# Second feed-forward layer: the seven-product form applied to two 512-token blocks at once, with one block's gated values kept in DRAM

## The chip, the cores and the metric

The program runs on one core of one Trainium2 chip. The metric is device time in microseconds (us) of one launch; lower is better. Matrix products run on TensorE (PE in the profile), elementwise work on VectorE (DVE), ScalarE (ACT) and GpSimd (POOL); SyncE (SP) issues nearly all DMAs of the part of the program that the change touches. Each of these engines works off its own instructions in order.

## The reference

```python
x = _attn_ref(x, state)                  # 8 batches, 512 tokens + 32 state rows each
x = x.transpose(...).reshape(4352, 512)  # 8 * 544 rows
g = x @ moe_w_gate; silu = g * (1 / (1 + np.exp(-g)))
x = (silu * (x @ moe_w_val)) @ moe_w_out             # layer 1, d_ff 1536
h = x @ moe2_w_in                                    # layer 2, d_ff 2048
g = h * (1 / (1 + np.exp(-1.702 * h)))
return (g @ moe2_w_out).astype(np.float32)
```

All is float32. The change touches layer 2 alone: `h = x @ w_in`, the gate, and `g @ w_out`, for 4352 rows.

## The kernel before, in words

**Precision.** A float32 operand is cut into a high and a low part (`cut`, L795 to L798: ACT casts the high part, DVE subtracts it for the low part). A product of two cut operands is three matmuls: high by high, low by high, high by low.

**Layer 2, by blocks.** The rows go through in nine blocks, called n here: n=0 holds the 256 state rows, n=1 to n=8 hold 512 tokens each. d_ff is cut into 16 strips f of 128 (`F2`). For each strip the kernel makes h, gates it, cuts the gated value (`to_h`, into one of three h tiles), and puts it on the list `waiting`; `out2` takes the oldest entry and adds its share of `g @ w_out` into four PSUM accumulators of 128 x 512 (`acc0` to `acc3`): 12 matmuls, 512 columns wide (L340 to L342). After the sixteenth strip of a block `evac` copies the accumulators out, two on ACT (L808) and two on DVE (L809), and SP stores them (L1209). The next block takes the same four accumulators.

**The seven products.** For n=0 and n=1 each strip is 12 plain matmuls. For n=2 to n=8 the function `four` makes two strips at once, as a 2 x 2 by 2 x 2 product with seven sub-products instead of eight (a Strassen-Winograd form). Rows of the weights are the two strips of a pair p (0 to 7), the shared dimension of 512 is halved, and the **columns are the two halves of the block's 512 tokens** (Q = 256). Each sub-product is six matmuls of 256 columns (L1230 to L1232), 42 for a pair. DVE and ACT add the seven results together from PSUM (L1240 to L1257), ACT takes the sigmoid (L1254, L1259), DVE multiplies (L1260, L1264). Two `out2` calls stand inside each `four`, after the fourth and after the seventh sub-product, so the output products of a block run between the sub-products of the same or the next block.

**Operands.** The seven token operands of block n+1 (plain quarters and differences of quarters) are made during block n by `x3_step`. Three of the weight operands are sums that were made once, during n=1; they come back from DRAM as chunks `w2c` (`next_chunk`, L1063, 512 KB, three slots), and the 16 strips of `w_out` come back for each block from `w2b` (`next_out`, L1053, 512 KB, three slots, each issued when the strip three places earlier has been used).

**Order.** It is written out by hand: the loops at the end of the program call `four`, `x3_step`, `out2` in sequence, and each engine's instructions stand in that order. Tiles with few buffers set who waits: PSUM has two `gv` and two `at` tiles, SBUF three `wt`, two `sg`, two `xf`, three h tiles, four `raw`.

Of the kernel before, what the change touches and what calls it, by code (L numbers as in the profile page):

```python
# [8 lines left out]
F32 = mybir.dt.float32  # L9
F32R = mybir.dt.float32r  # L10
U32 = mybir.dt.uint32
ACTF = mybir.ActivationFunctionType
ALU = mybir.AluOpType
# [61 lines left out]
def kernel(  # L75
# [24 lines left out]
    B, H, S, D = x.shape  # L100
    NS = state.shape[2]
    DM = H * D
    FF1 = w_gate.shape[1]
    FF2 = w2_in.shape[1]
    P = 128
# [3 lines left out]
    F2 = FF2 // P  # L109
# [6 lines left out]
    v, a, pe, pool_e, sy = nc.vector, nc.scalar, nc.tensor, nc.gpsimd, nc.sync  # L116
# [4 lines left out]
    work = ctx.enter_context(tc.tile_pool(name="work", bufs=2))  # L121
    xp = ctx.enter_context(tc.tile_pool(name="xop", bufs=1))
    dp = ctx.enter_context(tc.tile_pool(name="scratch", bufs=1, space=DRAM))
# [12 lines left out]
    def f32(t):  # L136
        return t.bitcast(F32)
# [17 lines left out]
    units = {}  # L155
    pos = {"dma": 0, "begun": 0, "done": 0, "ahead": 4, "outs": 0, "jobs": 0}
    RAWS = 4
# [155 lines left out]
    def need(key):  # L313
        while pos["done"] <= where[key]:
            w_step()
# [28 lines left out]
    def accs():  # L344
        return [psa.tile([P, 512], F32, name=f"acc{i}", tag=f"acc{i}") for i in range(4)]

    def gv():
        return psg.tile([P, 512], F32, name="gv", tag="gv")
# [3 lines left out]
    def at():  # L352
        if extra:
            extra.append(extra.pop(0))
            if extra[0] != "at":
                return psa.tile([P, 512], F32, name="at", tag=extra[0])
        return pst.tile([P, 512], F32, name="at", tag="at")
# [436 lines left out]
    y1 = {}  # L794

    def cut(h_, l_, src, eng=v):
        a.copy(h_, src)  # L797
        eng.tensor_tensor(l_, src, f32(h_), op=ALU.subtract)  # L798
# [2 lines left out]
        t = pl.tile([P, 2, S], F32R, name="xo", tag=f"x{k}")  # L801
        return t[:, 0, :N], t[:, 1, :N]

    def evac(acc, N):

        for e in range(0, len(acc), 2):
            ev = work.tile([P, 2, 512], F32, name="ev", tag="raw", bufs=RAWS)
            a.copy(ev[:, 0, :N], acc[e][:, :N])  # L808
            v.tensor_copy(ev[:, 1, :N], acc[e + 1][:, :N])  # L809
            yield e, ev  # L810

    def h_tile(n):
        pl = work if n < 2 else x2p
        return pl.tile([P, 2, 512], F32R, name="h", tag=f"h{n}", bufs=1)
# [44 lines left out]
    x2q = None  # L859
# [40 lines left out]
    order2 = [B] + list(range(B))  # L900
    for i, blk in enumerate(order1):
        tail = blk == B
        last = i == NB1 - 1
        N = NT if tail else S
# [26 lines left out]
        acc = []  # L931
# [39 lines left out]
        for f in range(F1):  # L971
# [4 lines left out]
            sg = work.tile([P, 512], F32, name="sg", tag="sg")  # L976
# [57 lines left out]
    Q = S // 2  # L1034
    PAIRS = F2 // 2
    NCH = 3 * PAIRS // 2
    chunks = [dp.tile([P, 2, 2, Q], F32, name=f"w2c{c}") for c in range(NCH)]
    XRAW = (6, 7)
    EXTRA = {0: (8, 9, 10), 1: (11, 12, 13)}

    def slot(f, shape, name, dt=F32R):
        pl, tag = slot2[f]
        return pl.tile(shape, dt, name=name, tag=tag, bufs=1)
# [13 lines left out]

    def next_chunk(load=True):
        c = pos2["chunks"]
        if c < NCH * (len(order2) - 1):  # L1060
            mixed[c] = t = slot(3 + c % 3, [P, 2, 2, Q], "wc")
            if load:
                sy.dma_start(f32(t), chunks[c % NCH])  # L1063
            pos2["chunks"] += 1

    def mixed_at(n, i):

        i += 3 * PAIRS * (n - 1)
        return mixed[i // 2][:, i % 2]
# [3 lines left out]
    def mix_load(p, late=False):  # L1073
        sraw[p] = r = work.tile([P, 2, DM], F32, name="sr", tag="raw", bufs=RAWS)
        for j in range(2):
            if late:
                sy.dma_start(r[:, j, :Q], whole2["i2", 2 * p + j][:, :Q])
            else:
                sy.dma_start(r[:, j, :], whole2["i2", 2 * p + j])
# [3 lines left out]
    def mix_store():  # L1083
        while full:
            c = full.pop(0)
            sy.dma_start(chunks[c], f32(mixed[c]))
# [36 lines left out]
    def mix_step(n, f):  # L1123

        mix_store()
        s = n * F2 + f
        for back, fn in ((2, mix_cut), (1, mix_add), (0, mix_load)):
            p, odd = divmod(s - back - 6, 2)
            if not odd and 0 <= p < PAIRS:
                fn(p)  # L1130
        if s == F2 + 8:
            for _ in range(3):
                next_chunk()
        for back, fn in ((2, late_cut), (1, late_add), (0, lambda p: mix_load(p, True))):
            p = s - back - F2 - 8
            if 0 <= p < PAIRS:
                fn(p)
# [4 lines left out]
    def x3_step(n, f):  # L1142

        if f == 1:
            for j in range(2):
                xraw[j] = r = slot(XRAW[j], [P, 2, S], "xr", F32)
                sy.dma_start(r, y1[order2[n]][j])
        if f < 3:
            return
        b11, b12 = xraw[0][:, :, :Q], xraw[0][:, :, Q:]  # L1150
        b21, b22 = xraw[1][:, :, :Q], xraw[1][:, :, Q:]
        ops = {
            3: (0, b11),
            4: (b11, b12, b11),
            5: (2, b22),
            6: (b12, b22, b12),
            7: (4, b11),
            8: (b11, b22, b11),
            9: (5, b11),
            10: (1, b21),  # L1160
            11: (b21, b11, b21),
            12: (6, b12),
            13: (3, b21),
        }
        op = ops.get(f)
        if op is None:
            return
        if len(op) == 3:
            v.tensor_tensor(op[0], op[1], op[2], op=ALU.subtract)
            return  # L1170
        k, src = op
        if k < 4 and (n % 2 or k < 2):
            t = (xp if n % 2 else x2q).tile([P, 2, 2, Q], F32R, name="xo", tag=f"x{k}")
        elif k < 4:
            t = slot(12 + k, [P, 2, 2, Q], "xo")
        else:
            t = slot(EXTRA[n % 2][k - 4], [P, 2, 2, Q], "xo")
        xs3.setdefault(n, {})[k] = t
        cut(t[:, 0], t[:, 1], src)

    waiting = []
    acc2 = {}
    done2 = {}

    def out2():
        n, f, h = waiting.pop(0)
        blk = order2[n]
        nt = (NT if blk == B else S) // P
        if n not in acc2:
            acc2[n] = accs()[:nt]  # L1190
            done2[n] = 0
        w = outs.pop((n, f)) if n else units["o2", f]
        done2[n] += 1
        for t in range(nt):
            c = slice(t * P, (t + 1) * P)
            mm_acc(acc2[n][t], h[:, 0, c], h[:, 1, c], w[:, 0, :], w[:, 1, :], done2[n] == 1, done2[n] == F2)
        if n:
            next_out()
        if done2[n] == F2:
            for t, ev in evac(acc2.pop(n), DM):  # L1200
                if blk == B:
                    per = P // NS
                    rows = out.rearrange("(b s) m -> b s m", s=SEQ)
                    for j in range(2):
                        b = (t + j) * per
                        sy.dma_start(rows[b : b + per, S:, :], ev[:, j, :])
                else:
                    rows = out[blk * SEQ : blk * SEQ + S, :].rearrange("(p j) m -> p j m", j=J)
                    sy.dma_start(rows[:, t : t + 2, :], ev)  # L1209
# [3 lines left out]
    def to_h(n, f, sg, N):  # L1213
        h = h_tile(count["h"] % 3)
        count["h"] += 1
        cut(h[:, 0, :N], h[:, 1, :N], sg[:, :N])
        waiting.append((n, f, h))

    def wt():
        return work.tile([P, 512], F32, name="wt", tag="wt", bufs=3)  # L1220
# [46 lines left out]
            if i % 2 == 1:  # L1267
                next_chunk()

    for n in range(len(order2)):  # L1270
        N = NT if order2[n] == B else S
        for f in range(F2):
            if n > 1:
                if n == 2:
                    mix_step(n, f)
                if f % 2 == 0:
                    four(n, f // 2)
                if n + 1 < len(order2):
                    x3_step(n + 1, f)
                continue  # L1280
            if n == 0:
                if 1 < f < 6:
                    need(("io"[f % 2] + "2", F2 - 3 + f // 2))
                if f == 8:
                    for _ in range(3):
                        next_out()
            ps = gv()
            mm_in(ps, units["i2", f], xs2[n], N)
            sg = work.tile([P, 512], F32, name="sg", tag="sg")
            a.activation(sg[:, :N], ps[:, :N], ACTF.Sigmoid, scale=1.702)  # L1290
            v.tensor_tensor(sg[:, :N], ps[:, :N], sg[:, :N], op=ALU.mult)
            to_h(n, f, sg, N)
            if n == 0:
                x2_step(1, f, 2)
            else:
                x3_step(2, f)
            mix_step(n, f)
            if len(waiting) > 2:
                out2()
    while waiting:  # L1300
        out2()

# [28 lines left out]
```

## Time and profile before

| | us |
|---|---|
| median of 3 runs | 1491.26 (1490.56 to 1491.71) |
| the profiled execution, its own time | 1492.28 |
| its span, first to last instruction | 1490.5 |
| PE busy in the span | 1467.6 (98%) |
| DVE / ACT / POOL busy | 915.6 / 684.2 / 396.1 |

The profile comes from one execution. Its span is 1.8 us shorter than that execution's time. A busy PE counts a matmul from its start to its modelled end; consecutive matmuls overlap, so how fast they follow one another is read from their start times. The blocks n=3 to n=8, which the change rewrites, fill about the last 500 us of the span; the granted TensorE clock is full there.

### The profile page before, as it was taken

The page shows a single profiled execution, that of the slowest core. Times are in us where ns is not written, and L with a number is a line of the kernel's source. Part 1 is how long each engine was busy: PE and PEld are TensorE (multiplying, and loading weights), DVE is VectorE, ACT ScalarE, POOL GpSimd, SP SyncE. Part 2 cuts the span into 40 slices and gives each one's busy share as a digit, 9 for nine tenths or more (in the row PEclk, how much of TensorE's full clock was granted, in tenths as well). Part 3 has the DMA queues.
Part 4 walks back from the last instruction along what each step waited for, and adds up shares of the span by engine and source line. Part 5 has one row for each costly group of instructions (what it writes and reads, how often), then busy time and mean ns, then how long its engine had stood idle before and what let it go on. Part 6 is the DMA issues. An engine that isn't in the chain of part 4 may idle for free.

```text
span 1490.5 us, 21226 instructions
## 1 busy us (share of the span) xinstructions
PE 1467.6 (98%) x7688; PEld 1193.8 (80%) x7688; DVE 915.6 (61%) x1600; ACT 684.2 (46%) x1247; POOL 396.1 (27%) x325
## 2 busy tenths in 40 slices
PE   7999999999999999999999999999999999999998
PEld 4445677777787777898788889999999999999997
DVE  7985565656678787943344335656565665656554
ACT  6766554555566666654444333333333232323322
POOL 2665221222234445477646330000000000000000
PEclk9999999999999999999999999999999999999999
DMA  7975433333365656425657746565654646574653
GB/s 217 292 248 159 133 99 110 108 125 105 126 189 172 197 170 190 130 100 171 207 189 270 261 147 211 180 232 174 209 198 170 240 159 240 178 240 165 207 183 128
DMA packets 138480, 269.30 MB, mean 181 GB/s; under 512 B 46728, under 2 KB 57992, under 8 KB 138376
## 3 DMA queue, kind: packets, MB, share of 16 engines
q1 hardware_dynamic: 114680, 223.64, 45.5%
q10 hardware_dynamic: 23696, 44.31, 8.9%
q8 instruction: 61, 1.00, 0.3%
q14 instruction: 43, 0.35, 0.1%
HBM read 202.11 MB, written 63.70 MB: 178 GB/s over the span
## 4 chain that ended last, share of the span: by engine, by line
PE 84%; DMA 5%; DVE 4%; ACT 3%; issue 2%; POOL 1%; SPq 0%; ACTq 0%; DVEq 0%; POOLq 0%
PE acc L340 8%; PE acc L341 8%; PE acc L342 8%; PE acc L952 5%; PE acc L954 5%; PE gv L330 5%; PE acc L953 5%; PE gv L331 4%; PE gv L332 4%; DMA xf<-sw 4%; PE gv L1232 4%; PE gv L1231 4%; PE gv L1230 4%; PE at L629 4%; PE at L1230 3%; PE at L1231 3%
## 5 line engine op out<-in xcount | busy, mean ns | idle before, releaser
L798 DVE TENSOR_TENSOR h<-sg,h 128x512 fp32r<-128x512 f32 (+1 forms) x240 | 193.5, 806 | 129.8 <-ACT h L797 128.2
L797 ACT CAST h<-sg 128x512 fp32r<-128x512 f32 (+1 forms) x251 | 149.8, 597 | 170.4 <-DVE sg L1264 80.2
L340 PE MATMUL acc<-wo,h 128*128 128x512 f32 x512 | 200.6, 392 | 0.0
L341 PE MATMUL acc<-wo,h 128*128 128x512 f32 x512 | 200.6, 392 | 0.0
L342 PE MATMUL acc<-wo,h 128*128 128x512 f32 x512 | 199.2, 389 | 0.0
L1254 ACT ACTIVATE sg<-wt 128x512 f32<-128x512 f32 x56 | 35.4, 632 | 299.5 <-DVE wt L1252 299.5
L668 POOL TENSOR_TENSOR xo<-xf,xo 128x512 fp32r<-128x512 f32 x84 | 110.9, 1325 | 231.9 <-ACT xo L667 216.5
L952 PE MATMUL acc<-h,wu 128*128 128x512 f32 (+1 forms) x428 | 165.9, 388 | 0.1
L954 PE MATMUL acc<-h,wu 128*128 128x512 f32 (+1 forms) x428 | 163.8, 383 | 2.0 <-DVE h L798 2.0
L953 PE MATMUL acc<-h,wu 128*128 128x512 f32 (+1 forms) x428 | 163.4, 382 | 0.0
L330 PE MATMUL gv<-a,xo 128*128 128x512 f32 x336 | 137.3, 409 | 0.0
L331 PE MATMUL gv<-a,xo 128*128 128x512 f32 x336 | 133.9, 399 | 0.6 <-POOL xo L668 0.5
L332 PE MATMUL gv<-a,xo 128*128 128x512 f32 x336 | 133.0, 396 | 0.0
L992 DVE TENSOR_TENSOR sg<-gv,sg 128x512 f32<-128x512 f32 (+1 forms) x107 | 70.5, 659 | 83.1 <-PE gv L332 50.7
L342 PEld LDWEIGHTS acc<-wo,h 128*128 128x128 f32 x512 | 96.2, 188 | 20.8
L340 PEld LDWEIGHTS acc<-wo,h 128*128 128x128 f32 x512 | 96.6, 189 | 17.1
L341 PEld LDWEIGHTS acc<-wo,h 128*128 128x128 f32 x512 | 96.6, 189 | 15.8
L1252 DVE TENSOR_TENSOR wt<-wt,gv 128x256 f32<-128x256 f32 x56 | 23.6, 421 | 136.4 <-PE gv L1232 136.4
L952 PEld LDWEIGHTS acc<-h,wu 128*128 128x128 f32 x428 | 80.9, 189 | 22.1 <-issue 6.1
L977 ACT ACTIVATE sg<-gv 128x512 f32<-128x512 f32 (+1 forms) x108 | 61.5, 570 | 80.1 <-PE gv L332 77.0
L954 PEld LDWEIGHTS acc<-h,wu 128*128 128x128 f32 x428 | 80.9, 189 | 21.1 <-DVE h L798 5.5
L1232 PE MATMUL gv<-xo,wu 128*128 128x256 f32 x336 | 95.4, 284 | 0.0
(178 smaller groups left out, 3438.6 us busy)
## 6 DMA issues: line engine op xcount, KB each, us to landing
wo<-w2b SPq DMA_DIRECT2D x128, 512.0 KB
wc<-w2c SPq DMA_DIRECT2D x84, 512.0 KB
xf<-sw ACTq DMA_DIRECT2D x84, 256.0 KB
raw<-in_moe_w_out_dram SPq DMA_DIRECT2D x28, 512.0 KB
sw<-qs ACTq DMA_DIRECT2D x24, 512.0 KB
sw<-qs ACTq DMA_DIRECT2D x24, 384.0 KB
xn<-in_x_dram SPq DMA_DIRECT2D x16, 512.0 KB
y<-ev SPq DMA_DIRECT2D x16, 512.0 KB
```

The source lines that it names most:

```text
L330: pe.matmul(ps, wh, xh, start=k == 0, stop=False)
L331: pe.matmul(ps, wl, xh, start=False, stop=False)
L332: pe.matmul(ps, wh, xl, start=False, stop=k == len(pairs) - 1)
L340: pe.matmul(ps, lh, rh, start=first, stop=False)
L341: pe.matmul(ps, lh, rl, start=False, stop=False)
L342: pe.matmul(ps, ll, rh, start=False, stop=last)
L797: a.copy(h_, src)
L798: eng.tensor_tensor(l_, src, f32(h_), op=ALU.subtract)
L952: pe.matmul(ps, w[:, 0, c], h[:, 0, :N], start=f == 0, stop=False)
L953: pe.matmul(ps, w[:, 1, c], h[:, 0, :N], start=False, stop=False)
L954: pe.matmul(ps, w[:, 0, c], h[:, 1, :N], start=False, stop=f == F1 - 1)
L1232: pe.matmul(ps, w[:, 0, c], x_[:, 1, kt], start=False, stop=kt == 1)
```

## The change

Blocks n=3 to n=8 go through as three pairs of blocks (`DUOS`); n=0, 1 and 2 stay as they were. In the new `four_duo` the **columns of the 2 x 2 product are the two blocks of a pair**, so each of the seven sub-products has six matmuls of 512 columns, and one call yields two strips for both blocks. The first block's gated values go to `to_h` and `out2` as before. The second block's are written to DRAM (`keep`, 256 KB each, L1339); after the eighth call `rest_of_duo` reads them back (L1386), cuts them, and runs the second block's sixteen `out2` with no sub-products between them. The token operands are made by `duo_step` on 1024 columns at a time (`x3_step` stays for n=2): for the first pair during n=2, for the others during `rest_of_duo`. The chunks of weight sums are read once for a pair of blocks. From n=2 on, `evac` uses tiles of another pool.

```diff
+            if late_out:
+                ev = x2q.tile([P, 2, 512], F32, name="ev", tag=f"x{e // 2}")
+            else:
+                ev = work.tile([P, 2, 512], F32, name="ev", tag="raw", bufs=RAWS)
...
+    DUOS = [(3, 4), (5, 6), (7, 8)]
...
-        if c < NCH * (len(order2) - 1):
+        if c < NCH * (2 + len(DUOS)):
...
+    HOME = {0: ("x0", "x1"), 5: ("x2", "x3"), 4: (6, 7), 6: (11, 12), 3: (13, 8), 1: (9, 10), 2: (14, 15)}
+    DUO_STEPS = [
+        (0, "11"),
+        ("11", "12", "11"),
...
+    def duo_load(j):
+
+        for k in range(2):
+            for c, n in enumerate(DUOS[j]):
+                r = work.tile([P, 2, S], F32, name="xr", tag="raw", bufs=RAWS)
+                sy.dma_start(r, y1[order2[n]][k])
...
+    def duo_step(i):
+
+        op = DUO_STEPS[i]
+        if len(op) == 3:
+            to, x_, y_ = (quarter[q] for q in op)
+            v.tensor_tensor(to, x_, y_, op=ALU.subtract)
+            return
...
+        cut(*parts, src)
...
+    def four_duo(j, p):
...
+        def prod(ps, w, k):
+            xh, xl = duo[k]
+            for kt in range(2):
+                c = slice(kt * P, kt * P + P)
+                pe.matmul(ps, w[:, 0, c], xh[:, kt], start=kt == 0, stop=False)
+                pe.matmul(ps, w[:, 1, c], xh[:, kt], start=False, stop=False)
+                pe.matmul(ps, w[:, 0, c], xl[:, kt], start=False, stop=kt == 1)
+            return ps
...
+        def keep(f, t, sg):
+            v.tensor_tensor(t, t, sg, op=ALU.mult)
+            held_h[nb, f] = d = dp.tile([P, S], F32, name=f"h_{nb}_{f}")
+            sy.dma_start(d, t)
...
+        ps = prod(gv(), s4, 2)
+        add_(one[1], ps, one[1], op=ALU.add)
+        if waiting:
+            out2()
+        to_h(na, 2 * p + 1, s_odd, S)
+        v.tensor_tensor(s_even, one[0], s_even, op=ALU.mult)
+        to_h(na, 2 * p, s_even, S)
+        sg = gated(one[1])
+        keep(2 * p, one[1], sg)
+        for i in range(3 * p + 3 * PAIRS * (j + 2), 3 * p + 3 + 3 * PAIRS * (j + 2)):
+            if i % 2 == 1:
+                next_chunk()
+
+    def rest_of_duo(j):
...
+        def read(s):
+            loaded.append(wt())
+            sy.dma_start(loaded[-1], held_h[nb, order[s]])
+
+        read(0)
+        read(1)
+        for s in range(F2):
+            if s + 2 < F2:
+                read(s + 2)
+            to_h(nb, order[s], loaded.pop(0), S)
+            if j + 1 < len(DUOS) and 0 < s <= len(DUO_STEPS):
+                duo_step(s - 1)
+            if len(waiting) > 2:
+                out2()
...
+                if f == 4:
+                    duo_load(0)
+                if 4 < f < 13:
+                    duo_step(f - 5)
...
+    for j in range(len(DUOS)):
+        for p in range(PAIRS):
+            four_duo(j, p)
+            if p == 4 and j + 1 < len(DUOS):
+                duo_load(j + 1)
+        rest_of_duo(j)
```

The change moves instructions at the place where a block's accumulators are handed to the next block. ACT before, where n=3 ends inside the first `four` of n=4: `h` casts are L797, `ev` copies L808.

```order
1047 L797 CAST h_8952<-sg_8931 128x512
1048 L1240 COPY wt_8959<-gv_8961 128x256
1049 L1254 ACTIVATE sg_9021<-wt_8960 128x512
1050 L1259 ACTIVATE sg_9031<-wt_8959 128x512
1051 L808 COPY ev_9048<-acc0_8269 128x512
1052 L808 COPY ev_9052<-acc2_8271 128x512
1053 L797 CAST h_9056<-sg_9021 128x512
```

ACT now, where n=3 ends in `rest_of_duo` of the first pair: `h_9908` and `h_9927` are the first two strips of n=4, cast from tiles that were read back; `xo_9930` is a token operand of the next pair of blocks; the `ev` copies are L811.

```order
1104 L797 CAST h_9890<-sg_9861 128x512
1105 L1333 ACTIVATE sg_9893<-wt_9788 128x512
1106 L797 CAST h_9908<-wt_9902 128x512
1107 L797 CAST h_9927<-wt_9904 128x512
1108 L797 CAST xo_9930<-xr_9551 128x1024
1109 L811 COPY ev_9948<-acc0_9133 128x512
1110 L811 COPY ev_9952<-acc2_9135 128x512
1111 L797 CAST h_9958<-wt_9906 128x512
```

The two `ev` copies of the finished block stood behind sigmoids of the running `four`; they now stand behind two casts whose inputs are DMA reads and one cast of 1024 columns. DVE has the same order.

SP's queue at the same place, before: `wo` are strips of `w_out`, `wc` chunks of weight sums, `xr` token rows.

```order
348 L1063 DMA wc_8955<-w2c1_6955 128x1024
349 L1063 DMA wc_8957<-w2c2_6956 128x1024
350 L1053 DMA wo_9004<-w2b0_134 128x1024
351 L1053 DMA wo_9046<-w2b3_137 128x1024
352 L1209 DMA out_0_dram<-ev_9048 128x1024
353 L1209 DMA out_0_dram<-ev_9052 128x1024
```

SP's queue now: `h_4_14` is strip 14 of n=4 on its way to DRAM, and the `wt` rows are the reads of strips 1, 0, 3 and 2.

```order
398 L1057 DMA wo_9884<-w2b1_135 128x1024
399 L1339 DMA h_4_14_9896<-wt_9788 128x512
400 L1067 DMA wc_9898<-w2c1_6955 128x1024
401 L1067 DMA wc_9900<-w2c2_6956 128x1024
402 L1386 DMA wt_9902<-h_4_1_9010 128x512
403 L1386 DMA wt_9904<-h_4_0_9087 128x512
404 L1386 DMA wt_9906<-h_4_3_9131 128x512
405 L1057 DMA wo_9923<-w2b0_134 128x1024
406 L1386 DMA wt_9925<-h_4_2_9204 128x512
407 L1057 DMA wo_9946<-w2b3_137 128x1024
408 L1213 DMA out_0_dram<-ev_9948 128x1024
```

The first read stands behind the write of the last strip and behind two chunks; in the third pair of blocks no chunk is left to load, and the two `wc` rows are missing there.

## Rows read from the trace of the kernel before

**Rows 1.** The page: its head, and part 1 (busy us by engine).
```profile
span 1490.5 us, 21226 instructions
PE 1467.6 (98%) x7688; PEld 1193.8 (80%) x7688; DVE 915.6 (61%) x1600; ACT 684.2 (46%) x1247; POOL 396.1 (27%) x325
```

**Rows 2.** Windows: PE, PEld, DVE, ACT, POOL busy, clock, DMA share, GB/s.
```profile
860.00:885.00 25.00, 25.00 (x112) 20.71 (x111) 9.19 (x13) 8.36 (x17) 7.23 (x8) 1.00 0.48 157
1000.00:1400.00 400.00, 400.00 (x2511) 362.65 (x2510) 242.16 (x482) 128.17 (x232) 0.00 (x0) 1.00 0.58 197
```

**Rows 3.** Timeline of SP's issues in n=1, and at ends of n=2, n=7.
```profile
864.44 0.32 SPq L1053 DMA_DIRECT2D wo<-w2b  x1
...
886.20 0.32 SPq L1053 DMA_DIRECT2D wo<-w2b  x1
...
986.68 0.86 SPq L1209 DMA_DIRECT2D out_dram<-ev  x2
...
1407.36 0.86 SPq L1209 DMA_DIRECT2D out_dram<-ev  x2
```

**Rows 4.** Timeline of PE (start, us): in n=4 of layer 2, then in layer 1.
```profile
1081.82 0.28 PE L1230 MATMUL gv<-xo,wc 128*128 128x256 f32 x1
...
1083.61 0.40 PE L340 MATMUL acc<-wo,h 128*128 128x512 f32 x1
...
564.00 0.40 PE L330 MATMUL gv<-a,xo 128*128 128x512 f32 x1
...
565.41 0.39 PE L952 MATMUL acc<-h,wu 128*128 128x512 f32 x1
```

**Rows 5.** Groups of ACT and DVE, 905 to 1400 us: busy, mean ns.
```profile
L798 DVE TENSOR_TENSOR h<-sg,h 128x512 fp32r<-128x512 f32 x95 | 65.8, 692 | 64.5 <-ACT h L797 64.5
L797 ACT CAST h<-sg 128x512 fp32r<-128x512 f32 x94 | 58.4, 621 | 68.8 <-DVE sg L1264 67.3
...
L1244 DVE TENSOR_TENSOR wt<-at,wt 128x256 f32<-128x256 f32 x48 | 20.4, 425 | 8.0 <-PE at L1232 3.6
...
L1240 ACT COPY wt<-gv 128x256 f32<-128x256 f32 x48 | 17.6, 366 | 2.0 <-PE gv L1232 2.0
...
L808 ACT COPY ev<-acc 128x512 f32<-128x512 f32 x10 | 5.8, 578 | 2.3 <-PE acc L342 1.8 <-issue 0.5
```

**Rows 6.** Timeline of DVE, then ACT, behind the program's last sub-product.
```profile
1479.65 0.69 DVE L798 TENSOR_TENSOR h<-sg,h 128x512 fp32r<-128x512 f32 x1 [0.69 <-ACT h L797]
1480.26 0.69 DVE L1264 TENSOR_TENSOR sg<-wt,sg 128x512 f32<-128x512 f32 x1
1481.69 0.69 DVE L798 TENSOR_TENSOR h<-sg,h 128x512 fp32r<-128x512 f32 x1 [0.74 <-ACT h L797]
...
1481.04 0.62 ACT L797 CAST h<-sg 128x512 fp32r<-128x512 f32 x1 [1.42 <-DVE sg L1264]
```

**Rows 7.** Timeline of DVE, then PE: a strip's low part, and its use.
```profile
1090.55 0.69 DVE L798 TENSOR_TENSOR h<-sg,h 128x512 fp32r<-128x512 f32 x1 [0.69 <-ACT h L797]
...
1094.59 0.39 PE L342 MATMUL acc<-wo,h 128*128 128x512 f32 x1
```

**Rows 8.** Chain that ended last: start, us, the DMA waited for (256 KB each).
```profile
72.43 2.84 DMA raw<-in_moe_w_gate_dram
...
783.29 3.56 DMA sr<-w2i
```

**Rows 9.** Windows early in the program (columns as in Rows 2).
```profile
14.00:16.00 2.00, 2.00 (x6) 0.68 (x4) 1.85 (x4) 2.00 (x4) 0.69 (x2) 1.00 1.05 385
```

**Rows 10.** Windows of PE alone: busy, count, granted clock, DMA share, GB/s.
```profile
78.00:80.00 2.00, 1.05 (x2) 1.00 0.13 45
80.00:82.00 2.00, 2.00 (x7) 0.69 0.87 242
82.00:84.00 2.00, 2.00 (x6) 0.50 0.87 231
84.00:86.00 2.00, 2.00 (x8) 0.96 0.99 355
472.00:474.00 2.00, 0.51 (x3) 1.00 0.43 152
```

More of the change, by code (lines that the diff above doesn't have):

```diff
@@ L802, in x_tiles, with evac @@
         return t[:, 0, :N], t[:, 1, :N]
-    def evac(acc, N):
+    def evac(acc, N, late_out=False):
         for e in range(0, len(acc), 2):
-            ev = work.tile([P, 2, 512], F32, name="ev", tag="raw", bufs=RAWS)
+            if late_out:
+                ev = x2q.tile([P, 2, 512], F32, name="ev", tag=f"x{e // 2}")
+            else:
+                ev = work.tile([P, 2, 512], F32, name="ev", tag="raw", bufs=RAWS)
             a.copy(ev[:, 0, :N], acc[e][:, :N])
@@ L1199, in out2 @@
         if done2[n] == F2:
-            for t, ev in evac(acc2.pop(n), DM):
+            for t, ev in evac(acc2.pop(n), DM, n > 1):
                 if blk == B:
@@ L1268, in four @@
                 next_chunk()
-    for n in range(len(order2)):
+    HOME = {0: ("x0", "x1"), 5: ("x2", "x3"), 4: (6, 7), 6: (11, 12), 3: (13, 8), 1: (9, 10), 2: (14, 15)}
+    DUO_STEPS = [
+        (0, "11"),
+        ("11", "12", "11"),
+        (4, "11"),
+        ("11", "22", "11"),
+        (5, "11"),
+        ("12", "22", "12"),
+        (6, "12"),
+        ("11", "11", "21"),
+        (3, "11"),
+        (1, "21"),
+        (2, "22"),
+    ]
+    duo = {}
+    quarter = {}
+    held_h = {}
@@ new lines, in duo_load @@
+    def duo_load(j):
[3 more added lines that the diff above has]
+                sy.dma_start(r, y1[order2[n]][k])
+                quarter[f"{k + 1}{c + 1}"] = r
+    def duo_step(i):
[4 more added lines that the diff above has]
+            return
+        k, src = op[0], quarter[op[1]]
+        parts = []
+        for home in HOME[k]:
+            if isinstance(home, str):
+                parts.append(xp.tile([P, 2, S], F32R, name="xo", tag=home))
+            else:
+                parts.append(slot(home, [P, 2, S], "xo"))
+        cut(*parts, src)
+        duo[k] = parts
@@ new lines, in four_duo, with gated @@
+    def four_duo(j, p):
+        na, nb = DUOS[j]
+        w0, w1 = units["i2", 2 * p], units["i2", 2 * p + 1]
+        def prod(ps, w, k):
[6 more added lines that the diff above has]
+            return ps
+        def gated(src):
+            sg = work.tile([P, 512], F32, name="sg", tag="sg")
+            a.activation(sg, src, ACTF.Sigmoid, scale=1.702)
+            return sg
+        def keep(f, t, sg):
+            v.tensor_tensor(t, t, sg, op=ALU.mult)
+            held_h[nb, f] = d = dp.tile([P, S], F32, name=f"h_{nb}_{f}")
+            sy.dma_start(d, t)
+        add_ = v.tensor_tensor
+        s2, s1, s4 = (mixed_at(3 + j, 3 * p + i) for i in range(3))
+        one = [wt(), wt()]
+        two = [work.tile([P, DM], F32, name="xf", tag="xf", bufs=2) for _ in range(2)]
+        ps = prod(gv(), w0[:, :, :Q], 0)
+        a.copy(one[0], ps)
+        ps = prod(at(), s2, 5)
+        add_(one[1], ps, one[0], op=ALU.add)
+        pb = prod(gv(), s1, 4)
+        ps = prod(at(), w1[:, :, :Q], 6)
+        add_(two[0], ps, one[1], op=ALU.add)
+        add_(two[1], pb, two[0], op=ALU.add)
+        add_(one[1], pb, one[1], op=ALU.add)
+        sg = gated(two[1])
+        keep(2 * p + 1, two[1], sg)
+        if waiting:
+            out2()
+        ps = prod(gv(), w1[:, :, Q:], 3)
+        add_(two[0], two[0], ps, op=ALU.subtract)
+        s_odd = gated(two[0])
+        ps = prod(at(), w0[:, :, Q:], 1)
+        add_(one[0], ps, one[0], op=ALU.add)
+        s_even = gated(one[0])
+        v.tensor_tensor(s_odd, two[0], s_odd, op=ALU.mult)
+        ps = prod(gv(), s4, 2)
+        add_(one[1], ps, one[1], op=ALU.add)
+        if waiting:
+            out2()
[7 more added lines that the diff above has]
+                next_chunk()
@@ new lines, in rest_of_duo @@
+    def rest_of_duo(j):
+        nb = DUOS[j][1]
+        order = [s ^ 1 for s in range(F2)]
+        loaded = []
+        def read(s):
[10 more added lines that the diff above has]
+            if len(waiting) > 2:
+                out2()
@@ L1271 @@
+    for n in range(3):
         N = NT if order2[n] == B else S
@@ L1273 @@
             if n > 1:
-                if n == 2:
-                    mix_step(n, f)
+                mix_step(n, f)
                 if f % 2 == 0:
                     four(n, f // 2)
-                if n + 1 < len(order2):
-                    x3_step(n + 1, f)
+                if f == 4:
+                    duo_load(0)
+                if 4 < f < 13:
+                    duo_step(f - 5)
+                if f == F2 - 1:
+                    for i in range(8, len(DUO_STEPS)):
+                        duo_step(i)
                 continue
```

## The prediction

> **What bounds the kernel now.** I read the page first: the span is 1490.5 us and PE is busy for 98% of it [rows 1]; the profiled execution took 1492.28 us, so 1.8 us lie around the span, and it stands 1.0 us above the median of 1491.26. Next the windows over the part that the change rewrites: from 1000 to 1400 us PE is busy for all 400, DVE for 242, ACT for 128, DMA at a share of 0.58 [rows 2]. Nothing is waited for on PE there, so what counts is how fast matmuls follow one another, and then every new place where PE waits. The timeline gives the paces. In n=7 SP stores the block before 420.68 us later than it did in n=3 (1407.36 less 986.68, five blocks) [rows 3]: **84.14 us a block**, for 336 matmuls of 256 columns and 192 of 512. Fifteen steps of 256 columns take 1083.61 - 1081.82 = 1.79 us, 0.1193 each [rows 4]. The pace of 512 columns in an unbroken stream stands in n=1, whose strips are 12 plain matmuls and 12 of `out2`, all 512 wide, from the same kinds of tiles, with PE busy throughout [rows 2]: four strips from 864.44 to 886.20 [rows 3], 5.44 us for 24 matmuls, **0.2267 each**. Two steps of 256 cost 0.2386, so the wide form is cheaper by 5% a column. The 84.14 us also show that the narrow stream taxes its neighbours: 336 x 0.1193 = 40.1 leaves 44.0 for 192 wide matmuls, 0.2294 each.
>
> **What the change removes.** Six blocks cost 6 x 84.14 = 504.8 us. Each pair of blocks becomes 8 x 42 = 336 products and 2 x 192 output matmuls, 720 in all, every one 512 wide: 3 x 720 x 0.2267 = 489.6. **PE gains 15.2 us** if it never waits. The DVE and ACT instructions on PSUM results halve in number and double in width; they had room (242 of 400) and get more. Half the chunk loads go; 48 writes and 48 reads of 256 KB come.
>
> **Inside `four_duo`** I charge nothing. A pair of strips now gives PE 66 x 0.2267 = 15.0 us, DVE 11 adds and multiplies and 2 low parts at 0.69 (13 x 0.69 = 9.0), ACT 7 instructions at about 0.62. Each PSUM tile is free before its next use, with a 5.4 us stretch of four sub-products and 2.7 us of `out2` between. If that cover failed it would show as a wait of a few tenths in each of 24 calls, up to 7 us.
>
> **During n=2** DVE and ACT get `duo_step` in place of `x3_step`, twice as wide. A strip's low part is ready at 1090.55 + 0.69 = 1091.24 and first used at 1094.59 [rows 7]: 3.35 us of cover, including a narrow x step. Width adds some 0.5 us to each instruction (below), two or three of them between uses, with a cast in their chain: up to 3 us. It still fits, barely. I take 0; bounds 0 and 4 us (half a us in each of eight calls).
>
> **The hand-over inside a duo** is the new cost. Call T the end of the last sub-product of the eighth `four_duo`. Before, a block's last `out2` was followed on PE by sub-products, and the copies of the accumulators ran under them. Now PE has three `out2` of the first block left, 36 x 0.2267 = 8.16 us, and then needs the second block's first strip and the freed accumulators.
> - DVE after T: the add of the last result (about T+0.2 to T+0.9), a low part and a multiply at steps of 0.61 (1479.65 to 1480.26 [rows 6]) to T+2.1; ACT casts strip 14 in 0.62 with 0.1 before it [rows 6], T+2.8; DVE its low part and the `keep` multiply, T+4.1. The write of strip 14 goes out at T+4.2, and SP, which is in order, comes to the two chunks and the reads only then: at 0.4 an issue, read 0 at T+5.5.
> - A single 256 KB transfer took 2.84 us from issue to landing, one behind another of its size 3.56 [rows 8]. At the best rate here, 385 GB/s [rows 9], 256 KB move in 0.68 and 512 KB in 1.36, so 2.16 of the 2.84 is lag. Write, two chunks and read 0 are 1.57 MB: T + 4.2 + 2.16 + 4.1 = T+10.4; read 1 lands at T+11.1.
> - ACT then casts strips 1 and 0 (to T+11.7), the 1024-wide `xo`, and only then copies `acc0`. 366 ns at 256 columns and 621 at 512 [rows 5] make 1.1 us at 1024 (bound: twice 0.62); the copy is 0.58 [rows 5], so `acc0` is free at T+13.35. PE waits 13.35 - 8.16 = 5.2 us. DVE (425 ns at 256, 692 at 512 [rows 5], so about 1.2 at 1024) copies `acc1` to T+14.65, 0.65 after PE wants it. **5.85 us each in the first two duos, 11.7.**
> - In the third, no chunk and no `xo` stand ahead: read 0 lands at T + 4.2 + 2.16 + 1.36 = T+7.7, read 1 at T+8.4, `acc0` is free at T+9.75: **1.6 us.**
>
> Sum 13.3. Its bounds: 3 us, if the reads were always in time and only the casts and copies counted (about 1 each), and 19, if the queue drained at 200 GB/s, nearest 1000 to 1400 us [rows 2]. I take 13.3 because the lag and the rate come from loads of this very size.
>
> **The rest of `rest_of_duo`.** Each 2.72 us step moves 512 KB of `w_out` and 256 KB of h, 289 GB/s, under the 385 seen. ACT needs 0.62 + 1.1 and DVE 0.69 + 1.2 a step at most. No wait charged.
>
> **The clock.** PE idle for 5 us can lower it. Early on, PE was busy for 1.05 of the 2 us from 78 to 80; the granted clock then went 0.69, 0.50, 0.96 [rows 10], which is 3.4 us at half speed (2.4 to 1.2 GHz). From 472 to 474, busy 0.51 of 2, nothing fell. Waits of 5.2 us are far longer than either, so I expect a fall after each of the first two and none after 1.6 us. 3.4 us at half speed lose at most 1.7; part of it passes while PE waits, so 1.3 each, **2.6 us** (bounds 0 and 6.8, if it stays low twice as long). The Trainium skill says of this ("TensorE: Matmul & The Clock Gate", Part 1) that the throttled state is the default and activity releases it; rows 10 show both outcomes. By that rule the term stays; without it the sum would be 2.6 us lower.
>
> **Sum.** -15.2 + 13.3 + 2.6 = +0.7 us: the profiled execution would be 1493.0, the median **1492.0**.
>
> **Rivals.**
> - *The transfers keep ahead, and the clock holds: faster.* If read 0 does not queue behind the two chunks (2 x 1.36 = 2.7 us earlier in two duos, 5.4) and the clock doesn't fall (2.6), the time is 1492.0 - 8.0 = 1484. For it: the share of 0.58 leaves the engines idle at times, and 472 to 474 passed without a fall. Against it: SP's order puts the chunks ahead, and all go through one queue. 0.17.
> - *The width pays little: slower.* In layer 1 six products of 512 columns took 565.41 - 564.00 = 1.41, 0.235 each [rows 4]. If `four_duo`'s 1008 products had that pace, they would cost 8.4 us more: 1500. It decides from about 0.229 a step upward. Against it: n=1 has the same weights and tiles as `four_duo`, at 0.2267. 0.13. The Trainium skill's formula for back-to-back matmuls ("TensorE: Matmul & The Clock Gate", "Back-to-back issue gap": columns / 2.4 + 2.5 ns) points the same way: 109.2 and 215.8 ns, by which 24 calls would save only about 2.6 us (an estimate by that page) and the time would be near 1505. The traces' 119.3 and 226.7 ns disagree with it.
> - *`rest_of_duo` is bound by its transfers: slower by far.* At the 200 GB/s of n=3 to n=7 [rows 2] a step would take 3.9 us instead of 2.72, 48 steps 57 us: 1549. Against it: that rate is what was asked for, at a share of 0.58. 0.05.
>
> **Chances.** My forecast 0.55 (own range 1488 to 1495.5); faster rival 0.17; little pay 0.13; transfer-bound 0.05; the remaining 0.10 is a longer low clock or waits in n=2 and `four_duo`, 1494 to 1500. The range of eight in ten, 1486 to 1499, takes in most of these. About 0.2%, 3 us, is what can be told from no change here. Faster: 0.05 of mine and 0.15 of the rival, 0.20. Slower: 0.08 of mine, 0.13, 0.05 and 0.05, 0.31. Within: 0.49.
>
> **What would show it.** Products L1326 to L1328 stepping at 0.227 and 15.0 us a call; PE idle before the first L340 of n=4 and n=6 for about 5 us and released by ACT's `ev` copy L811, of n=8 for 1.6; after the first two a stretch at clock 0.50; n=2 still at 84 us. I am wrong if PE steps at 0.235 there, if the waits are under 3 us or over 8, or if waits recur inside `rest_of_duo`.

## Result, and the profile after

The changed kernel takes **1499.91 us** (median of 5 runs, 1497.56 to 1502.95) against 1491.26 for the kernel before (5 runs, 1489.96 to 1491.71): a ratio of **1.0058**, 95% interval 1.0047 to 1.0069. It is slower by 8.65 us. The prediction was 1492.0 with a range of 1486 to 1499, so the time lies just outside, and 7.9 us above the forecast. The profiled execution took 1498.6 us.

The page of the kernel after, its head and its table of busy time (us, share, instructions), answers to [rows 1]:

```profile
span 1496.8 us, 19040 instructions
PE 1458.8 (97%) x6680; PEld 1144.1 (76%) x6680; DVE 897.2 (60%) x1399; ACT 677.5 (45%) x1202; POOL 396.6 (26%) x325
```

PE has 1008 matmuls less (each two narrow ones became one wide one) and is busy for 8.8 us less, yet the span is 6.3 us longer. So PE stands idle, or steps more slowly, for more than the products saved. Spans also differ outside the change: in the profile of before the clock fell at 81 us [rows 10], in this one it did not fall there, and the store of block n=1 came 1.8 us earlier. From that store, where the changed part begins, to the last store the two profiles read as follows (SP's timeline, kernel after):

```profile
900.74 0.85 SPq L1213 DMA_DIRECT2D out_dram<-ev  x2
...
1491.87 1.69 SPq L1213 DMA_DIRECT2D out_dram<-ev  x2
```

That is 591.13 us; in the trace of before the same two issues stand at 902.58 and 1485.39, 582.81 us apart. The changed part is 8.3 us longer, which agrees with the 8.65 of the medians.

First, the products. The windows of the kernel after, with columns as in [rows 2], while n=2 makes operands for the first duo and then over six calls of `four_duo`:

```profile
905.00:980.00 75.00, 75.00 (x456) 66.96 (x456) 48.38 (x86) 26.80 (x42) 0.00 (x0) 1.00 0.62 216
1000.00:1090.00 90.00, 90.00 (x398) 74.53 (x398) 51.30 (x78) 25.26 (x43) 0.00 (x0) 1.00 0.55 182
```

SP's timeline there shows the writes of the second block's even strips, one for each call.

```profile
1057.55 0.32 SPq L1339 DMA_DIRECT2D h<-xf  x1
1072.51 0.32 SPq L1339 DMA_DIRECT2D h<-xf  x1
1087.47 0.32 SPq L1339 DMA_DIRECT2D h<-xf  x1
```

PE is never idle in these windows, and a call with its 66 matmuls takes 14.96 us: 0.2267 each, the pace taken from n=1 [rows 3]. So the gain is real. What eats it stands in the table of PE's waits (us in total, times, longest), of which the kernel before has nothing in this stretch [rows 2]:

```profile
PE acc L340 <- ACT ev L811: 15.0, 3, 6.2
PE acc L340 <- DMA wo<-w2b: 0.6, 1, 0.6
```

Three waits for the accumulator's copy, one in each duo. PE's timeline around the first, then the first matmul after each of the others:

```profile
1099.10 0.39 PE L342 MATMUL acc<-wo,h 128*128 128x512 f32 x1
1105.70 0.79 PE L340 MATMUL acc<-wo,h 128*128 128x512 f32 x1 [6.21 <-ACT ev L811]
1106.29 0.63 PE L341 MATMUL acc<-wo,h 128*128 128x512 f32 x1
1106.72 0.63 PE L342 MATMUL acc<-wo,h 128*128 128x512 f32 x1
...
1109.14 0.40 PE L342 MATMUL acc<-wo,h 128*128 128x512 f32 x1
1109.37 0.39 PE L340 MATMUL acc<-wo,h 128*128 128x512 f32 x1
...
1276.98 0.79 PE L340 MATMUL acc<-wo,h 128*128 128x512 f32 x1 [6.00 <-ACT ev L811]
...
1446.09 0.50 PE L340 MATMUL acc<-wo,h 128*128 128x512 f32 x1 [2.79 <-ACT ev L811]
```

The bracket says what ended the idle time. The second column shows a further loss: behind the wait a matmul takes 0.63 us instead of 0.39, and starts are 0.43 apart (1106.29, 1106.72) instead of 0.23 (1109.14, 1109.37). That is the clock. Windows of the same place, all engines, with the granted clock third from the end:

```profile
1098.00:1100.00 2.00, 1.49 (x7) 0.91 (x5) 0.00 (x0) 0.00 (x0) 0.00 (x0) 1.00 0.91 332
1100.00:1102.00 2.00, 0.00 (x0) 0.00 (x0) 0.00 (x0) 0.00 (x0) 0.00 (x0) 1.00 1.02 398
1102.00:1104.00 2.00, 0.00 (x0) 0.00 (x0) 0.38 (x1) 1.02 (x2) 0.00 (x0) 0.50 1.01 398
1104.00:1106.00 2.00, 0.30 (x1) 0.30 (x2) 1.75 (x3) 2.00 (x4) 0.00 (x0) 0.50 0.40 78
1106.00:1108.00 2.00, 2.00 (x5) 1.35 (x5) 2.00 (x4) 0.65 (x2) 0.00 (x0) 0.50 0.97 365
1108.00:1110.00 2.00, 2.00 (x8) 1.58 (x8) 1.35 (x2) 0.00 (x0) 0.00 (x0) 0.79 1.02 401
```

From 1100 to 1102 no engine computes at all and the DMA engines are full at 398 GB/s: everything waits for the queue. The clock is at half (1.2 GHz) from 1102.0, 6.8 us long, and PE works in the last 3.1 of them. At the second hand-over the records show 6.8 us from 1276.1, nearly all of it with PE at work again (it restarts at 1276.98); at the third 3.4 us from 1446.7. PE's own windows, with the clock after the count:

```profile
1272.00:1278.00 6.00, 1.02 (x3) 0.84 0.86 325
1278.00:1284.00 6.00, 6.00 (x17) 0.59 0.87 290
1446.00:1450.00 4.00, 3.91 (x10) 0.59 0.88 275
```

Why the first wait is as long as it is stands in two more timelines, SP's and then ACT's:

```profile
1088.19 6.21 SPq L1057 DMA_DIRECT2D wo<-w2b  x2
1095.35 0.32 SPq L1339 DMA_DIRECT2D h<-wt  x1
1095.71 0.94 SPq L1067 DMA_DIRECT2D wc<-w2c  x2
1096.75 2.30 SPq L1386 DMA_DIRECT2D wt<-h  x3
```

```profile
1102.97 1.24 ACT L797 CAST h<-wt 128x512 fp32r<-128x512 f32 x2 [8.44 <-DMA wt<-h]
1104.12 1.04 ACT L797 CAST xo<-xr 128x1024 fp32r<-128x1024 f32 x1
1105.07 1.07 ACT L811 COPY ev<-acc 128x512 f32<-128x512 f32 x2
```

T, the end of the last sub-product, is about 1091.2. The last write goes out at T+4.1, the chunks and the reads behind it, and ACT can cast the first strip read back at 1102.97, 6.2 us after that read's issue. Two casts and the 1024-wide one stand ahead of the copies of the accumulators, which PE finished with at 1099.5.

Adding up every start-to-start distance on PE from 880 us on, beyond its own pace (0.2267 and 0.1195), the kernel before loses 3.2 us and the kernel after 23.9: waits 15.6, the slow steps behind the three hand-overs 6.5 (1.65, 2.95 and 1.9), n=2 0.5, and 1.3 in small pieces. With the 15.2 gained this is +8.7. Strictly, the 0.5 us that the kernel before loses in n=1 and n=2 has to come off (the other 2.7 of its 3.2 lie in the six blocks and are in the 15.2 already). That leaves +8.2, close to the 8.3 between the two stretches from store to store.

### The profile page after: what moved, and what is told of

The parts are those of the page before. It is cut to its first block, busy times and chain, and to the rows that moved or that the text cites. A ratio compares the mean times of both kernels' runs of the same rounds, so it can differ in the third digit from the quotient of the medians.

```text
span 1496.8 us, 19040 instructions
## 1 busy us (share of the span) xinstructions
PE 1458.8 (97%) x6680; PEld 1144.1 (76%) x6680; DVE 897.2 (60%) x1399; ACT 677.5 (45%) x1202; POOL 396.6 (26%) x325
## 4 chain that ended last, share of the span: by engine, by line
PE 81%; DMA 7%; DVE 5%; ACT 3%; issue 2%; POOL 1%; SPq 1%; ACTq 0%; POOLq 0%; DVEq 0%
PE acc L340 8%; PE acc L341 8%; PE acc L342 8%; PE gv L330 5%; PE acc L957 5%; PE acc L955 5%; PE gv L331 5%; PE acc L956 5%; PE gv L332 4%; DMA xf<-sw 3%; PE at L629 3%; PE gv L1326 3%; PE gv L1327 3%; PE gv L1328 3%; PE at L1326 2%; PE at L1327 2%
## 5 line engine op out<-in xcount | busy, mean ns | idle before, releaser
L340 PE MATMUL acc<-wo,h 128*128 128x512 f32 x512 | 203.0, 396 | 15.6 <-ACT ev L811 15.0
L798 DVE TENSOR_TENSOR h<-sg,h 128x512 fp32r<-128x512 f32 (+1 forms) x192 | 162.3, 845 | 81.7 <-ACT h L797 80.0
L797 ACT CAST h<-sg 128x512 fp32r<-128x512 f32 (+1 forms) x203 | 120.0, 591 | 138.6 <-DVE sg L995 71.1
L340 PEld LDWEIGHTS acc<-wo,h 128*128 128x128 f32 x512 | 97.5, 190 | 38.8 <-ACT ev L811 16.3
L342 PEld LDWEIGHTS acc<-wo,h 128*128 128x128 f32 x512 | 97.4, 190 | 21.2 <-DVE h L798 0.4
L341 PEld LDWEIGHTS acc<-wo,h 128*128 128x128 f32 x512 | 97.8, 191 | 19.2
L1333 ACT ACTIVATE sg<-xf 128x512 f32<-128x512 f32 x48 | 30.4, 633 | 178.1 <-DVE xf L1352 113.5
L957 PEld LDWEIGHTS acc<-h,wu 128*128 128x128 f32 x428 | 80.5, 188 | 22.5 <-DVE h L798 7.1
L955 PEld LDWEIGHTS acc<-h,wu 128*128 128x128 f32 x428 | 80.6, 188 | 21.8 <-issue 6.1
L956 PEld LDWEIGHTS acc<-h,wu 128*128 128x128 f32 x428 | 80.6, 188 | 15.6 <-POOL wu L251 0.3
L330 PEld LDWEIGHTS gv<-a,xo 128*128 128x128 f32 x336 | 63.2, 188 | 30.6 <-issue 18.2
```

The costliest lines, as they stand in the source:

```text
L330: pe.matmul(ps, wh, xh, start=k == 0, stop=False)
L340: pe.matmul(ps, lh, rh, start=first, stop=False)
L341: pe.matmul(ps, lh, rl, start=False, stop=False)
L342: pe.matmul(ps, ll, rh, start=False, stop=last)
L955: pe.matmul(ps, w[:, 0, c], h[:, 0, :N], start=f == 0, stop=False)
L956: pe.matmul(ps, w[:, 1, c], h[:, 0, :N], start=False, stop=False)
```

## Experiments

Theory A, the prediction's own: the loss is the hand-over (copies of the accumulators queued behind casts that wait for the read-back), and the clock that falls because PE is idle there. Rival B: the loss is in the DMA queue itself, so that mending the order on ACT only makes the next transfer, the strips of `w_out`, the one that is late. All ratios are against the kernel before, run on the same chip: median 1492.01 us for the first four, 1492.4 for the last two. Each experiment's own note has its own theories A and B.

**The accumulators copied before anything that waits.** All of the first block's `out2` run ahead of the loop, so `evac` stands before the casts.

```diff
         read(1)
+        while waiting:
+            out2()
         for s in range(F2):
```

> The two out2 calls left of the first block, and with them the copies of its accumulators, are written ahead of the casts of the strips that were read back. Theory A (order): PE's waits of 6.2, 6.0 and 2.8 us are made of two parts, the landing of read 0 and the casts that stand ahead of the copies. Then only read 0 and one cast are left: 4.2, 4.2 and 1.9 us, released by the cast (L797) and not by the copy (L811), and the time falls by 4.7 us of waits and 0 to 3 us of low clock, to 1492 to 1495. Theory B (the read alone decides, the copies come in time anyway): waits and time as in the changed kernel, 1499 to 1501.

1497.23 us, ratio 1.0035 (1.0023 to 1.0047). ACT's timeline, and the table of PE's waits:

```profile
1101.29 0.59 ACT L811 COPY ev<-acc 128x512 f32<-128x512 f32 x1 [2.96 <-PE acc L342]
...
1107.41 0.62 ACT L797 CAST h<-wt 128x512 fp32r<-128x512 f32 x1 [4.18 <-DMA wt<-h]
```

```profile
PE acc L340 <- ACT h L797: 12.4, 4, 4.8
```

The copies now run as soon as PE is done, and PE waits for the cast instead, that is for the read. So the order on ACT was worth about 1.5 us in each of the first two duos, and the transfer the rest. In the third duo the wait shrinks to 1.17 us, but a new one of 2.17 us comes up some steps later. The time lies between the two theories: the waits fell by 3.2 us in all and not by 4.7, and the waits of 4.8 and 4.3 us are still followed by 6.8 us at half clock each, the one of 2.17 by 3.4, so nothing is saved there. (The profiled execution took 1500.69 us, the second slowest of the 12; the trace shows more loss than the median has.)

**The chunks of the next duo later.** The two chunk loads that stand ahead of the reads move to the fourth step of the loop.

```diff
+        if p < PAIRS - 1:
+            chunks_of(j, p)
...
+            if s == 3:
+                chunks_of(j, PAIRS - 1)
```

> The two chunk loads that stand ahead of read 0 in SP's queue are issued later, in the fourth step of rest_of_duo. Theory A (one queue, served in order): read 0 lands 2.5 to 3 us earlier in the first two pairs of blocks, whose waits shrink from 6.2 and 6.0 to about 3.3 us; the third (no chunks there) stays at 2.8. Time 1492 to 1495. Theory B (reads are served beside the chunks, and the lag is the write to DRAM ahead of them): waits unchanged, 1499 to 1501.

1496.11 us, ratio 1.0023 (1.0011 to 1.0035). The table of PE's waits:

```profile
PE acc L340 <- ACT ev L811: 9.6, 3, 3.9
PE acc L340 <- DMA wo<-w2b: 3.6, 3, 1.6
```

The first two waits fall to 3.35 and 3.91, by 2.9 and 2.1 us: the two chunks were worth about what they take on the queue (2.7 by the prediction's rate). But 3.6 us of waits for `w_out` appear: 1.32 and 0.68 behind the place where the chunks were put, and 1.60 in the third duo, which has no chunks. So theory A is right about the reads, but the time is 1.1 us above its range: the queue is late with something else, as rival B says.

**PE kept busy through the wait.** Unread 512-column matmuls (26, 26 and 11) into a free PSUM tile, issued just before the second block's first strip. They compute nothing that is used.

```diff
+            if s == 1:
+                ps = gv()
+                reps = 11 if j == 2 else 26
+                for r in range(reps):
+                    pe.matmul(ps, units["i2", 0][:, 0, :P], duo[2][0][:, 0], start=r == 0, stop=r == reps - 1)
```

> Between the last out2 of the first block and the first out2 of the second, PE gets 26, 26 and 11 matmuls of 512 columns whose result nobody reads (5.9, 5.9 and 2.5 us), so that it works where it waited. Theory A (the clock falls because PE idles there): no stretch at clock 0.50 in layer 2, the wait at the place under 1 us, and the time falls by the 6 us or so that PE now loses at half speed, to 1492 to 1495, with less spread between runs. Theory B (the clock falls for another reason, or costs nothing here): 1499 to 1501.

1496.24 us, ratio 1.0031 (1.002 to 1.0042). PE's windows over the first two hand-overs:

```profile
1098.00:1104.00 6.00, 6.00 (x28) 1.00 0.95 326
1104.00:1110.00 6.00, 5.53 (x23) 1.00 0.85 310
1272.00:1278.00 6.00, 5.88 (x27) 1.00 0.84 314
1278.00:1284.00 6.00, 5.58 (x24) 1.00 0.97 342
```

The clock stays at 1.00 through all three hand-overs, though the data come as late as before: the first strip read back is cast 5.9 us after its read's issue, against 6.2. Over whole executions the mean granted clock was 0.994 to 0.998 in these 12 runs and 0.989 to 0.992 in the five of the changed kernel. So the clock fell because PE was idle, not because of anything else in this stage. Its fall costs 0.0058 - 0.0031 of the time, about 4 us, and by the two intervals anything from 2 to 6. From the trace it is 5.4: the kernel loses 4.2 us beyond its pace, its 63 extra matmuls cost 63 x 0.2267 = 14.3, and 23.9 - 18.5 = 5.4. The time is 1.2 us above theory A's range, and the spread between runs did not shrink (6.1 us over 12 runs, 5.4 over the five).

**The strips made last used first.** Strips 15 and 14 of the second block stay in SBUF and are the first two that it uses; the other 14 go through DRAM. Nothing then has to come back at the hand-over.

```diff
+            if f >= F2 - 2:
+                held_h[nb, f] = t
+                return
...
+        for f in strips(nb)[:2]:
+            to_h(nb, f, held_h[nb, f], S)
+            out2()
+        for s in range(F2 - 2):
```

> The second block's last two strips (15 and 14) stay in SBUF and are the first that rest_of_duo casts and uses; the other fourteen are written and read back as before, and are needed 5.4 us later. Theory A (the hand-over is all that stands between the 15 us gain of the wide products and the clock): no wait over 1 us on PE at the three places, no fall of the clock, 1475 to 1479, faster than the kernel before by 12 to 16 us. Theory B (waits move into the next steps of rest_of_duo, because reads and w_out strips share the queue): PE waits again for reads or strips there, 1485 to 1496.

1487.09 us, ratio **0.9965** (0.9952 to 0.9978): faster than the kernel before. No hand-over is at half clock. What is left, in the table of waits, then SP's timeline at the first hand-over:

```profile
PE acc L340 <- DMA wo<-w2b: 6.6, 5, 2.0
```

```profile
1097.30 0.89 SPq L1074 DMA_DIRECT2D wc<-w2c  x2
1098.29 0.92 SPq L1396 DMA_DIRECT2D wt<-h  x2
1099.64 3.04 SPq L1064 DMA_DIRECT2D wo<-w2b  x2
1102.77 0.86 SPq L1220 DMA_DIRECT2D out_dram<-ev  x2
```

The wait for the read-back and all three falls of the clock are gone, as theory A said, so both were due to the hand-over. But the time lies in theory B's range, 8 us above A's, and B's sign is there too: 6.6 us of waits for strips of `w_out`, up to 1.96 long. At the first two hand-overs their loads were issued behind 1 MB of chunks and 512 KB of reads, and the next ones stand behind the stores of the first block's result; in the third duo, without chunks, one wait of 1.79 us comes some steps later. The queue of rival B is the second limit, under the first.

**The same, with the transfers spread.** On top of the last kernel, the first block's two stores are issued in steps 4 and 6 of the loop, the two chunk loads in steps 8 and 10.

```diff
+                    if n > 2 and n % 2 == 1:
+                        put_off.append((rows[:, t : t + 2, :], ev))
+                    else:
+                        sy.dma_start(rows[:, t : t + 2, :], ev)
...
+            if s in (4, 6):
+                sy.dma_start(*put_off.pop(0))
+            if s == 8 or s == 10:
+                next_chunk()
```

> As the kernel with the last two strips first (e4), and the bulk transfers are taken out of the hand-over: the first block's two output stores are issued in the fifth and seventh step of rest_of_duo's loop, the two chunk loads in the ninth and eleventh. In e4 PE still waited 6.6 us in all, released by w_out strips that had queued behind chunks, stores and reads. Theory A (the queue is backed up only at the hand-over, and drains later at its 290 GB/s of 400): these waits go, under 1 us is left in all, and the time is 5 to 7 us below e4's, ratio to the kernel before 0.991 to 0.993. Theory B (the queue has no room anywhere in rest_of_duo): the waits move to the later steps, ratio as e4's, 0.995 to 0.998.

1481.92 us (1477.78 to 1484.19), ratio **0.9922** (0.9906 to 0.9938): by the medians 10.5 us faster than the kernel before, by the ratio 11.6. By the two ratios that is some 20 us faster than the changed kernel. Its table of waits, and a window of 45 us over PE's first hand-over:

```profile
PE acc L340 <- DMA wo<-w2b: 2.0, 5, 0.8
PE acc L340 <- ACT h L797: 0.5, 1, 0.5
```

```profile
1090.00:1135.00 45.00, 43.91 (x191) 35.14 (x189) 28.70 (x35) 19.37 (x28) 0.00 (x0) 1.00 0.84 286
```

PE is idle for 1.1 us of these 45, at full clock, while the DMA engines move 286 GB/s. The ratio is in theory A's range, but 2.5 us of waits remain where it allowed 1: 2.0 for `w_out`, in the later steps where the second store and the chunks now stand, and 0.5 in n=2. Of the 15.2 us that the wide products gain, 10.5 arrive.

**No read-back at all.** The changed kernel, with the casts reading a part of the weights that lies in SBUF instead of strips from DRAM. It leaves out the second block's true values; writes, chunks, `w_out` and stores stay.

```diff
-        read(0)
-        read(1)
         for s in range(F2):
-            if s + 2 < F2:
-                read(s + 2)
-            to_h(nb, order[s], loaded.pop(0), S)
+            to_h(nb, order[s], f32(units["i2", 0][:, 0, :]), S)
```

> The changed kernel without the reads of the second block: rest_of_duo casts a tile that lies in SBUF (a part of the weights) instead of the strips, so the second block's output is not that of the reference; the writes to DRAM stay, and so does the order of casts and copies. Theory A (the transfers behind SP's queue are the whole loss, the wide products give their 15 us): no wait over 0.5 us at the three places, no low clock in layer 2, ratio to before 0.989 to 0.991. Theory B (part of the loss is in four_duo, in the 1024-column casts or in the order of the copies): waits of 1 us and more remain, ratio 0.993 or above.

1485.04 us, ratio 0.9953 (0.9936 to 0.9971). PE's waits:

```profile
PE acc L340 <- DMA wo<-w2b: 3.4, 2, 1.9
```

With the reads gone PE never waits for ACT or DVE: the copies, casts and 1024-wide steps by themselves cost nothing, so the causes that theory B named here are out. The clock does not fall in layer 2. What is left are 1.5 and 1.9 us for `w_out` at the two hand-overs that have chunks and none at the third, which has none. So theory A's "no wait over 0.5 us" failed as well, and the ratio is 0.004 above its range: rival B's share of the loss, the queue, stays without any read-back.

The traces (one execution each) and the ratios of all seven kernels agree within 3.1 us: the loss beyond PE's own pace less 15.2 (and plus 14.3 for the extra matmuls) gives +8.7 for the changed kernel, then +7.0, +6.5, +3.3, -6.5, -9.1 and -9.5 us in the order of the experiments; the ratios give +8.7, +5.2, +3.4, +4.6, -5.2, -11.6 and -7.0. Three of the gaps have a plain reason in part: the profiled executions of the first and second experiments took 3.5 and 2.1 us more than their medians, that of the last 2.7 less.

## Why the prediction was wrong, by its own steps

- **The products: right.** 0.2267 us each and 14.96 us a call, as predicted; the gain of 15.2 closes the sum above. The rival in which width pays little is out, and with it the formula of the Trainium skill ("TensorE: Matmul & The Clock Gate", "Back-to-back issue gap"; the section gives it for isolated matmuls) as a guide to this stream: it gives 215.8 ns where the changed kernel, with a weight load for every matmul, steps at 226.7. One slip in the working changes nothing: the store at 1407.36 falls in n=8, not in n=7, which is what makes it five blocks.
- **Inside `four_duo`, n=2, and the rest of `rest_of_duo`: nearly right.** No wait in `four_duo`; n=2 cost 0.5 us, inside its bounds of 0 to 4. The 1024-wide instructions were sized well: 1.04 us for the cast above, against 1.1. The steady part of `rest_of_duo` shows PE busy throughout at 288 GB/s, against 289 predicted, so the transfer-bound rival is out as well:

```profile
1112.00:1137.00 25.00, 25.00 (x111) 20.33 (x110) 16.86 (x18) 10.36 (x14) 0.00 (x0) 1.00 0.89 288
```

- **The hand-over: place, releaser and order right, size 2 us short.** 13.3 was predicted, 15.0 measured, and 0.6 for `w_out` in the third duo. Up to the write (T+4.1 against T+4.2) the working holds; the read then landed 1.3 us later than it said (cast at T+11.8 against T+10.5). The sum of what drains ahead of the read left out the strip of `w_out` issued at 1094.08, the second of SP's pair at 1088.19, but by the sum's own rate and lag that moves the landing by 0.1 us only (1094.08 + 2.16 + 5.45 = 1101.7 against 1101.6). What the sum had wrong is the rate: it took 385 GB/s throughout, and the windows show 309 from 1096 to 1098 and 332 from 1098 to 1100, some 0.7 us of the 1.3; the rest is open. The waits were 6.2, 6.0 and 2.8 us against 5.85, 5.85 and 1.6. That the first two agree so well is partly luck: 0.65 of the 5.85 was a second wait, for DVE's copy, which does not show. PE at half clock came to `acc1` at 1107.14, just after the copy was done (about 1107.0); with PE kept busy, at full clock, two such waits of 0.41 and 0.42 us come up. So the part that was forecast for ACT's copy was 5.2 and measured 6.2 and 6.0. And the bound of 19 for a queue at 200 GB/s comes to 22 to 24 by its own steps.
- **The clock: the step that failed.** "I expect a fall after each of the first two and none after 1.6 us. 3.4 us at half speed lose at most 1.7 [...] so 1.3 each, 2.6 us." The third wait, 2.8 us long, brought a fall too, and the first two lasted 6.8 us, not 3.4. The slow steps cost 6.5 us by the start times, and the experiment with extra matmuls puts the term at 4 to 5.4. The bound of 6.8 was in the text ("if it stays low twice as long"), but the range took almost nothing of it, and none of the signs of being wrong that the prediction names is about how long the clock stays low. The evidence behind 3.4 was one fall after half-busy work [rows 10], when PE went on working. The trace of the kernel before also had a fall twice as long: in the five windows of 2 us from 18 to 28 us the granted clock was 0.83, 0.50, 0.50, 0.50 and 0.96, which is 6.8 us at half, with PE waiting about 1 us at a time. Nothing said that the shorter one was the one to count with. At the hand-over PE stood quite still for up to 6.2 us, and how much of the low stretch falls on PE's restart is decided by where it lies. At the second hand-over 5.9 of 6.8 us came after it.
- **The faster rival** needed the reads to keep ahead of the chunks and the clock to hold. Neither happened by itself; where the last two strips stayed in SBUF, PE did not wait for the reads and the clock held, and the time went below the rival's 1484 us once the other transfers were spread.

With the measured sizes in its places the sum is -15.2 + 15.6 + 6.5 + 0.5 = +7.4, and 1.3 in small pieces: the error was in the sizes, 2.3 us in the waits and 3.9 in the clock, both on the same side. With the 5.4 or the 4 of the extra matmuls in place of 6.5, the clock's error is 2.8 or 1.4; what was missed is the same by each, a fall after the third wait and slow stretches of 6.8 us instead of 3.4.

Two things stay open. In the third duo, read 0 took 4.75 us from issue to cast with one write and one strip of `w_out` ahead of it; SP, ACT and windows (columns as in [rows 2]):

```profile
1439.15 0.32 SPq L1339 DMA_DIRECT2D h<-wt  x1
1439.58 3.09 SPq L1386 DMA_DIRECT2D wt<-h  x3
```

```profile
1444.33 1.22 ACT L797 CAST h<-wt 128x512 fp32r<-128x512 f32 x2 [6.00 <-DMA wt<-h]
```

```profile
1440.00:1442.00 2.00, 2.00 (x10) 1.66 (x9) 0.00 (x0) 0.00 (x0) 0.00 (x0) 1.00 1.00 311
1442.00:1444.00 2.00, 1.30 (x6) 0.75 (x4) 0.00 (x0) 0.00 (x0) 0.00 (x0) 1.00 0.72 256
```

Their 1 MB at 398 GB/s and the lag of 2.16 us make 4.8 from the issue of the strip at 1437.89, so until 1442.7, 1.6 us too early. The transfers were slower than that: 117 GB/s from 1438 to 1440, then the 311 and 256 of the windows, by which the 1 MB has only just moved at 1442.7, before any lag of landing. Why they were slower here than the 398 of the first hand-over, no run tried. And the last 4.7 us of the 15.2 that the best version does not get were not taken apart beyond the 2.5 us of waits in its table.

## What to carry to other kernels

When a change fuses two stages, look at the one point where data made last is wanted first: what was hidden under the other stage is bare there, and everything queued ahead on SP and on the copying engine counts. Use first what was made last and is still on chip, and keep bulk loads and stores from lining up at that point. Price a PE wait of several us with its clock behind it: here 15 us of waits brought another 4 to 6.5.

## What the hardware showed that was not expected

- A wait of 2.79 us was enough for the clock to fall to half, for 3.4 us; waits of 6.0 and 6.2 brought 6.8 us each, and one of 4.3 us (first experiment, second hand-over) 6.8 as well. With the chunks late, a wait of 3.35 brought 6.8 and one of 3.91 brought 3.4. One of 2.17 (first experiment, third duo, with one of 1.17 eight us before it) brought 3.4, while one of 2.37 (chunks late, third duo) and one of 1.96 (last strips first) brought none. So the length of a wait gave neither the length of the slow stretch nor, near 2 us, whether there was one.
- Matmuls whose result nobody reads held the clock at 1.00 through a 6 us wait, and the kernel with them was faster by 0.0058 - 0.0031 of the time, 4 us with 2 to 6 by the intervals.
- A 256 KB read that shared its queue with loads issued up to 2.7 us earlier took 6.2 us from issue to use, against 2.84 from issue to landing for one alone [rows 8].
